# Pooled attention and a GELU feed-forward on one core: load shapes of v, order of the first batch's steps, order of the weight loads, and the last output tile in two parts

## The chip, the cores and the metric

The kernel runs on one core of a Trainium2 chip. The metric is the device time of one launch in microseconds. TensorE (PE in the profile) does the matmuls and the transposes, VectorE (DVE) and ScalarE (ACT) work on what it leaves in PSUM, and GpSimd (POOL) and SyncE (SP) mostly issue DMAs. ACT issues some DMAs as well.

## The reference

```python
# q, k, v: [8 batches, 8 heads, 576, 64] float32; w_in [512, 2048], w_out [2048, 512] float32
k_p = k.reshape(B, H, 72, 8, D).mean(axis=3)          # 8 neighbouring rows pooled
v_p = v.reshape(B, H, 72, 8, D).mean(axis=3)
scores = np.matmul(q, k_p.transpose(0, 1, 3, 2)) / np.sqrt(D)
attn = np.exp(scores - scores.max(-1)); attn /= attn.sum(-1)
x = np.matmul(attn, v_p).transpose(0, 2, 1, 3).reshape(4608, 512)
h = x @ w_in
g = 0.5 * h * (1 + np.tanh(c * (h + 0.044715 * h**3)))
out = g @ w_out                                        # [4608, 512] float32
```

## The kernel before

The 4608 rows of x are cut into nine groups of 512 (`GROUP`), and the attention of batch b + 1 is computed while group b goes through the feed-forward, so that x is always ready in SBUF, transposed, as `xT` (four blocks of 128 of its 512 features, `ko`, by 4608 rows). The schedule is written by hand: every engine works through its instructions in the order in which the program lists them.

**A group.** `p1_mm` (L336) computes h transposed, 16 blocks `fo` of 128 features with four matmuls of 512 columns each; `gelu` (L342, ACT) writes each block to `gT`. `p2_mm` (L345) multiplies four row tiles `r` of 128 rows by `w_out_b`, 16 matmuls of 512 columns each. `store` copies a row tile from its PSUM bank to SBUF on DVE (L350) and issues four output DMAs of 32 partitions by 2 KB (L356) on SP; for the very last row tile two of the four go out on ACT's queue. Between the `p2_mm` of a group stand the score matmuls (`qk`, L239), exponentials (`expo`, L247), value matmuls (`av`, L261) and divisions (`norm`, `mult`) of the next batch. In group 0 the first two row tiles use `w_out_b` a quarter at a time, eight matmuls for each quarter, because `w_out_b` is still arriving.

**The first batch** has no group to hide behind. Its steps stand ahead of group 0: pooling k (`k_steps`, L139), transposing k and q, the scores and exponentials of its eight half-batches, the pooling of v (`v_steps(0)`, L139, which adds the eight rows of each pool and writes `vz`), the denominators (`den0`, L289: matmuls with a block of ones), their reciprocals on ACT (`inverse0`, L294 and L296), the outputs (`av0`, L304, which reads `vz`) and the multiplication into `xT` on DVE (`mult0`, L308). `spin(n, bank)` (L362) puts n matmuls of zeros into a bank, whose only effect is on TensorE's time and clock. After the last `mult0` the matmuls of group 0 start.

**Loads.** `load_v(b, engs)` brings the first 64 of the 72 pools of each head to `vts`: 128 partitions, of which the lower 64 hold heads 0 to 3 and the upper 64 heads 4 to 7, with four slots of 512 values (8 rows of 64) in each. Before the change it is two DMAs of 64 partitions by four slots, the source being walked in the order pool, head, values. `load_k` brings k to `kts` and, with two small DMAs of 32 partitions (L76), the remaining eight pools of v, whose source is walked in the order pool (8), head (4), values. For batch 0, SP and ACT issue these loads. All other loads are issued by POOL, in this order: q of batch 0 in two halves, `w_in_b` in two halves (the DMA casts to bf16), k of batch 1 with its small parts (four DMAs), q of batch 1, v of batch 1 (two DMAs), the four quarters of `w_out_b`, then q of batch 2. Later batches are loaded by `load_next`, one per group.

Of the kernel before, what the change touches and what calls it, by code (L numbers as in the profile page):

```python
# [8 lines left out]
F32 = mybir.dt.float32  # L9
# [9 lines left out]
def kernel(  # L19
# [9 lines left out]
    nc = tc.nc  # L29
    B, H, S, D = q.shape  # L30
    Sp = S // 8
    N = B * S
    DM = H * D
    DF = moe_w_in.shape[1]
    KO = DM // 128
    FO = DF // 128
    T = S // 32
    TP = T // 2
    CH = S // 2
    GROUP = 512  # L40
    NG = N // GROUP
# [11 lines left out]
    opool = ctx.enter_context(tc.tile_pool(name="op", bufs=6))  # L53
# [4 lines left out]
    PS = psp.tile([128, 8, 512], F32, name="PS")  # L58
# [4 lines left out]
    vts = [consts.tile([128, 4, 512], F32, name=f"vt{i}") for i in range(2)]  # L63
# [12 lines left out]
            engs[-1].dma_start(out=kts[b % 2][32 * i:32 * i + 32, KR], in_=rows[64:, 4 * i:4 * i + 4])  # L76

    def load_v(b, engs):
        rows = v[b].rearrange("h (j l) d -> j h (l d)", l=8)
        for i in range(2):  # L80
            engs[i % len(engs)].dma_start(out=vts[b % 2][64 * i:64 * i + 64], in_=rows[0:64, 4 * i:4 * i + 4])  # L81

    def load_q(b, i0=0, i1=2):
        if b not in qs:
            qs[b] = qp.tile([128, 2, T * D], BF16, name="qb")
        nc.gpsimd.dma_start(  # L86
            out=qs[b][:, i0:i1],
            in_=q[b].rearrange("(i h) (p t) d -> (h p) i (t d)", i=2, t=T)[:, i0:i1])
# [3 lines left out]
    w_out_b = consts.tile([128, FO, DM], BF16, name="w_out_b")  # L92
# [15 lines left out]
    load_w_in(1)  # L108
    load_k(1, [nc.gpsimd])
    load_q(1)  # L110
    load_v(1, [nc.gpsimd])
    for i in range(4):
        nc.gpsimd.dma_start(out=w_out_b[:, 4 * i:4 * i + 4, :].rearrange("p j d -> p (j d)"), in_=w_out_v[:, i])  # L113
    gate = consts.tile([1, 2], BF16, name="gate")

# [81 lines left out]
    def trans_k(b, bank):  # L197
        trans_k_mm(b, bank)
        for e in range(2):
            trans_k_copy(b, e, bank)  # L200
# [31 lines left out]
    def pool_rows(pr):  # L232
        return Sp if pr < PR // 2 else 128
# [49 lines left out]
    def den0(c, pr, bank):  # L283
        for x in range(2):
            e = es[0, c, pr + x]
            n = pool_rows(pr)
            for y in range(2):
                one = ones[:n, pr // 2].rearrange("j a d -> j (a d)")[:, 64 - 64 * y:192 - 64 * y]
                nc.tensor.matmul(out=PS[:, bank + x, :CH], lhsT=one, rhs=e[:n, y, :],  # L289
                                 start=(y == 0), stop=(y == 1))  # L290

    def inverse0(c, pr, bank):
        ld = ep.tile([128, 2, CH], F32, name="ld0", bufs=1)
        nc.scalar.activation(out=ld, in_=PS[:, bank:bank + 2, :CH], func=ACT.Ln)  # L294
        rc = ep.tile([128, 2, CH], F32, name="rc0")
        nc.scalar.activation(out=rc, in_=ld, func=ACT.Exp, scale=-1.0)  # L296
        rcs[0, c, pr] = rc

    def av0(c, pr, bank):
        for x in range(2):  # L300
            e = es.pop((0, c, pr + x))
            n = pool_rows(pr)
            for y in range(2):
                nc.tensor.matmul(out=PS[:, bank + x, :CH], lhsT=window(vz[:n], 2 * (pr + x) + y),  # L304
                                 rhs=e[:n, y, :], start=(y == 0), stop=(y == 1))

    def mult0(c, pr, bank):
        nc.vector.tensor_tensor(out=xT[:, pr:pr + 2, c * CH:(c + 1) * CH], in0=PS[:, bank:bank + 2, :CH],  # L308
                                in1=rcs.pop((0, c, pr)), op=ALU.mult)
# [3 lines left out]
    def act_set(name):  # L313
        nc.scalar.preload_act_table_set(name)  # L314


    def x_bank(g):
        return g % 2
# [9 lines left out]
    def o_bank(g, r):  # L328
        return 1 - x_bank(g) if r % 2 == 0 else x_bank(g)

    gTs = {}
# [9 lines left out]
            gTs[g] = gpool.tile([128, FO, GROUP], BF16, name="gT")  # L341
        nc.scalar.activation(out=gTs[g][:, fo, :], in_=PS[:, h_bank(g, fo), :], func=ACT.Gelu_apprx_tanh)  # L342

    def p2_mm(g, r, fo):
        nc.tensor.matmul(out=PS[:, o_bank(g, r), :], lhsT=gTs[g][:, fo, r * 128:(r + 1) * 128], rhs=w_out_b[:, fo, :],  # L345
                         start=(fo == 0), stop=(fo == FO - 1))

    def store(g, r):
        osb = opool.tile([128, DM], F32, name="osb")
        nc.vector.tensor_copy(out=osb, in_=PS[:, o_bank(g, r), :])  # L350

        for n in range(4):
            b, c = divmod(g * GROUP + r * 128 + n * 32, S)
            rows = out[b * S:(b + 1) * S].rearrange("(p t e) d -> e t p d", t=TP, e=2)
            eng = nc.scalar if (g, r) == (NG - 1, 3) and n % 2 else nc.sync
            eng.dma_start(out=rows[c // CH, c % CH // 32], in_=osb[n * 32:(n + 1) * 32, :])  # L356


    def spin(n, bank):

        for _ in range(n):
            nc.tensor.matmul(out=PS[:, bank, :], lhsT=idle[:, 0:128], rhs=idle, start=True, stop=True)  # L362
# [24 lines left out]
    for h in range(H):  # L387
        i = h // 4
        nc.tensor.matmul(out=PS[64 - 64 * i:72 - 64 * i, 7, h * D:(h + 1) * D],
                         lhsT=identb[0:64, 32 * i + h % 4:32 * i + 32:4], rhs=kps[0][0:64, KR],  # L390
                         start=True, stop=True)
# [3 lines left out]
    for i in range(2):  # L395
        p = slice(64 - 64 * i, 72 - 64 * i)
        nc.vector.tensor_copy(out=vz[p, 4 * i:4 * i + 4, 0],
                              in_=PS[p, 7, 256 * i:256 * i + 256].rearrange("p (h d) -> p h d", d=D))
# [9 lines left out]
    for f in v_steps(0):  # L408
        f()
    inverse0(1, 0, 6)  # L410
    spin(4, 4)
    av0(0, 0, 4)
    mult0(0, 0, 4)
    den0(0, 2, 2)
    inverse0(0, 2, 2)
    av0(1, 0, 0)
    mult0(1, 0, 0)
    spin(3, 6)
    den0(1, 2, 6)
    inverse0(1, 2, 6)  # L420
    spin(3, 4)
    av0(0, 2, 4)
    mult0(0, 2, 4)
    spin(3, 0)
    av0(1, 2, 0)
    mult0(1, 2, 0)
    for t in kps:
# [12 lines left out]
    for g in range(NG):  # L440
        nb = g + 1 if g + 1 < B else None
        act_set(GELU_SET)

        def load_next():

            load_q(g + 2)
            trans_q_dma(g + 2)
            nc.gpsimd.tensor_copy(out=gate, in_=qTs[g + 2][0:1, 1, TP - 1, 0:2])  # L448
            load_k(g + 2, [nc.gpsimd])
            load_v(g + 2, [nc.gpsimd])  # L450

        if 0 < g and g + 2 < B:
            load_next()


        side = {fo: [] for fo in range(FO)}
        if nb is not None:
            kk = k_steps(nb)
            tk = [lambda: trans_k(nb, 4)]
            kk.append(lambda: v_moves(nb))  # L460
            vv = v_steps(nb)
            if g:
                plan = {2: kk[:1], 3: kk[1:], 7: vv[:1], 8: vv[1:], 9: tk}
            else:
                tq = [lambda a=a, i=i: trans_q(nb, *a, (5, 6, 7, 5)[i], nc.vector) for i, a in enumerate(QG)]
                plan = {0: kk, 12: tq[:1], 13: tq[1:2] + tk, 14: tq[2:3], 15: tq[3:] + vv}
            for fo, what in plan.items():
                side[fo] += what

        if g == 0:
            first = [(fo, ko) for ko in (2, 3) for fo in range(4)]
        else:
            late = 3
            rest = [fo for fo in range(4) if fo != late]
            first = [(fo, ko) for ko in range(3) for fo in rest]
            first += [(late, ko) for ko in range(3)]
            first += [(fo, 3) for fo in rest + [late]]
        for fo, ko in first:  # L480
            p1_mm(g, fo, ko)
        for fo in range(FO):
            if fo >= 4:
                for ko in range(KO):
                    p1_mm(g, fo, ko)
            gelu(g, fo)
            for s in side[fo]:
                s()

        if g == 0:  # L490
            load_next()


        todo = {}

        def at(m, f, *a):
            todo.setdefault(m, []).append((f, a))

        if nb is not None:
            act_set(EXP_SET)  # L500
            pos = (6, 14, 20, 27, 34, 41, 48, 55, 61)
            for i in range(len(ORDER) + 1):
                if i < len(ORDER):
                    at(pos[i], qk, nb, *ORDER[i], 2)
                if i:
                    a = (nb, *ORDER[i - 1], 4 + 2 * ((i - 1) % 2))
                    at(pos[i], av, *a)
                if i < len(ORDER):
                    at(pos[i], expo, nb, *ORDER[i], 2)
                if i:  # L510
                    at(pos[i], norm, *a)
                    at(min(pos[i] + 9, 62 if i < len(ORDER) else 65), mult, *a)
        seq = [(r, fo) for r in range(4) for fo in range(FO)]
        if g == 0:

            seq[:32] = [(r, 4 * f4 + f) for f4 in range(4) for r in range(2) for f in range(4)]
        for m, (r, fo) in enumerate(seq):
            for f, a in todo.pop(m, []):
                f(*a)
            p2_mm(g, r, fo)  # L520
            if fo == FO - 1:
                store(g, r)
        for m in sorted(todo):
            for f, a in todo[m]:
                f(*a)


# [28 lines left out]
```

The softmax here doesn't subtract the row's maximum and nothing guards it: scores larger than these inputs give would overflow.

## Time and profile before

| what | value |
|---|---|
| median of three runs | 308.79 us (308.76 to 308.96) |
| the profiled execution's own time | 308.29 us |
| its span, first to last instruction | 306.5 us |
| TensorE busy | 298.2 us (97%), 1518 matmuls |
| ACT, DVE, POOL busy | 219.0, 150.4, 36.3 us |
| DMA | 41.12 MB, mean 134 GB/s |
| first matmul of group 0 | 22.08 us |
| group 0, group 1, group 2, from first matmul to first matmul of the next | 33.70, 31.84, 31.84 us |

The profile is of one execution. Its own time is 1.79 us longer than its span, which is what lies before the first and after the last instruction, and it is 0.50 us below the median of the three runs. Times inside the profile are counted from the start of the span. A busy time of 97% on TensorE counts matmuls that overlap and the matmuls of zeros as well, so it is no measure of useful work; where the span can be shortened is read from what TensorE waits for and from the work that it does for no result.

### The profile page before, as it was taken

The page shows a single profiled execution, that of the slowest core. Times are in us where ns is not written, and L with a number is a line of the kernel's source. Part 1 is how long each engine was busy: PE and PEld are TensorE (multiplying, and loading weights), DVE is VectorE, ACT ScalarE, POOL GpSimd, SP SyncE. Part 2 cuts the span into 40 slices and gives each one's busy share as a digit, 9 for nine tenths or more (in the row PEclk, how much of TensorE's full clock was granted, in tenths as well). Part 3 has the DMA queues.
Part 4 walks back from the last instruction along what each step waited for, and adds up shares of the span by engine and source line. Part 5 has one row for each costly group of instructions (what it writes and reads, how often), then busy time and mean ns, then how long its engine had stood idle before and what let it go on. Part 6 is the DMA issues. An engine that isn't in the chain of part 4 may idle for free.

```text
span 306.5 us, 4325 instructions
## 1 busy us (share of the span) xinstructions
PE 298.2 (97%) x1518; PEld 157.4 (51%) x1548; DVE 150.4 (49%) x334; ACT 219.0 (71%) x402; POOL 36.3 (12%) x69
## 2 busy tenths in 40 slices
PE   8999999999999999999999999999999999999994
PEld 3555555555555555555555555555555555445441
DVE  5868557573677057806681559245933630110021
ACT  1686679868987798779977998789868987206400
POOL 7103002305004000220014000400000000000000
PEclk9999999999999999999999999999999999999999
DMA  7999996987957952596159725662101210121022
GB/s 225 266 257 253 214 186 137 299 176 177 269 146 167 247 122 51 114 282 156 34 112 266 168 56 106 200 151 71 35 1 36 63 41 2 34 70 34 2 70 68
DMA packets 30359, 41.12 MB, mean 134 GB/s; under 512 B 18113, under 2 KB 18113, under 8 KB 29441
## 3 DMA queue, kind: packets, MB, share of 16 engines
q0 software_dynamic: 7856, 25.43, 34.9%
q1 hardware_dynamic: 21888, 14.09, 19.2%
q10 hardware_dynamic: 592, 1.31, 1.2%
q8 instruction: 12, 0.20, 0.3%
q14 instruction: 11, 0.08, 0.1%
HBM read 36.70 MB, written 9.44 MB: 151 GB/s over the span
## 4 chain that ended last, share of the span: by engine, by line
PE 83%; DMA 12%; POOL 1%; issue 1%; ACT 0%; DVE 0%; POOLq 0%
PE PS L345 38%; PE PS L336 36%; DMA kt<-in_k_dram 7%; DMA w_out_b<-in_moe_w_out_dram 5%; PE PS L239 4%; PE PS L261 4%; PE PS L174 1%; POOL w_in_b L105 0%; POOL qb L86 0%; POOL w_out_b L113 0%; DVE osb L350 0%; ACT e L247 0%; ACT ld L269 0%; ACT ld L268 0%; POOL identb masks.py:199 0%
## 5 line engine op out<-in xcount | busy, mean ns | idle before, releaser
L345 PE MATMUL PS<-w_out_b,gT 128*128 128x512 bf16 x560 | 134.2, 379 | 0.9
L336 PE MATMUL PS<-xT,w_in_b 128*128 128x512 bf16 x563 | 126.2, 379 | 0.6
L342 ACT ACTIVATE gT<-PS 128x512 bf16<-128x512 f32 x144 | 81.1, 604 | 47.5 <-PE PS L336 47.4
L336 PEld LDWEIGHTS <-w_in_b 128*128 128x128 bf16 x576 | 64.7, 113 | 57.2
L345 PEld LDWEIGHTS <-gT 128*128 128x128 bf16 x576 | 56.1, 97 | 56.7 <-issue 1.1
L350 DVE COPY osb<-PS 128x512 f32<-128x512 f32 x36 | 24.9, 691 | 98.3 <-PE PS L345 95.3
L279 DVE TENSOR_TENSOR xT<-PS,rc 64x288 bf16<-64x288 f32 x112 | 51.0, 455 | 31.6 <-ACT rc L271 29.3
L247 ACT ACTIVATE e<-PS 72x576 bf16<-72x576 f32 (+1 forms) x64 | 41.0, 646 | 9.1 <-PE PS L239 8.2
L239 PE MATMUL PS<-qT,kT 128*72 128x288 bf16 (+1 forms) x128 | 25.9, 286 | 0.9 <-ACT qT L214 0.6
L271 ACT ACTIVATE rc<-ld 128x288 f32<-128x288 f32 x56 | 24.8, 443 | 1.8
L314 ACT ACT_TABLE_LOAD x17 | 21.8, 1283 | 4.3 <-issue 4.1
L268 ACT ACTIVATE ld<-PS 64x288 f32<-64x288 f32 x56 | 22.8, 407 | 1.3
L269 ACT ACTIVATE ld<-PS 64x288 f32<-64x288 f32 x56 | 22.5, 402 | 1.3
L261 PE MATMUL PS<-e,vp 72*128 72x288 bf16 (+1 forms) x112 | 23.1, 286 | 0.0
L139 DVE TENSOR_TENSOR kt<-kt 128x1280 f32<-128x1280 f32 (+5 forms) x18 | 18.8, 1044 | 5.5 <-DMA kt<-in_v_dram 2.6
L239 PEld LDWEIGHTS <-kT 128*72 128x72 bf16 (+1 forms) x128 | 13.2, 105 | 15.2 <-DVE qT L216 1.2
L448 POOL COPY gate<-qT 1x2 bf16<-1x2 bf16 x6 | 1.0, 174 | 140.0 <-DMA qT<-qb 140.0
L139 DVE TENSOR_TENSOR vt<-vt 128x1024 f32<-128x1024 f32 (+1 forms) x16 | 15.3, 956 | 1.8 <-DMA vt<-in_v_dram 1.5
L184 DVE COPY kT<-PS 64x288 bf16<-64x288 bf16 (+2 forms) x48 | 13.0, 319 | 6.2 <-PE PS L174 6.1
L362 PE MATMUL PS<-idle 128*128 128x512 bf16 x39 | 11.9, 447 | 1.2 <-DVE idle L127 1.2
L261 PEld LDWEIGHTS <-vp 72*128 72x128 bf16 (+1 forms) x112 | 11.0, 98 | 3.8
L81 POOL DMA_DIRECT2D vt<-in_v_dram x14 | 9.0, 655 | 7.5 <-DMA w_in_b<-in_moe_w_in_dram 5.5
(47 smaller groups left out, 90.0 us busy)
## 6 DMA issues: line engine op xcount, KB each, us to landing
out_dram<-osb SPq DMA_DIRECT2D x142, 64.0 KB
kt<-in_k_dram POOLq DMA_DIRECT2D x7, 1024.0 KB, 6.2
vt<-in_v_dram POOLq DMA_DIRECT2D x14, 512.0 KB, 8.6
qb<-in_q_dram POOLq DMA_DIRECT2D x7, 576.0 KB, 11.6
w_in_b<-in_moe_w_in_dram POOLq DMA_DIRECT2D x2, 1024.0 KB, 16.7
w_out_b<-in_moe_w_out_dram POOLq DMA_DIRECT2D x4, 512.0 KB, 13.9
kt<-in_k_dram POOLq DMA_DIRECT2D x7, 128.0 KB, 5.9
kt<-in_v_dram POOLq DMA_DIRECT2D x14, 64.0 KB, 5.7
```

Of the source, the lines that this page charges most:

```text
L139: nc.vector.tensor_tensor(out=o, in0=a, in1=b, op=ALU.add)
L239: nc.tensor.matmul(out=PS[:n, bank + e, :CH].rearrange("j (t p) -> j t p", p=32), lhsT=kTs[b % 2][c][:, h, :n], rhs=qTs[b][:, h // 4, :, h ...
L247: nc.scalar.activation(out=e[:n], in_=PS[:n, bank:bank + 2, :CH], func=ACT.Exp, scale=1.0 / 64.0)
L261: nc.tensor.matmul(out=PS[:, bank + x, :CH], lhsT=window(vps[b % 2][:n], 2 * pr + x), rhs=e[:n, x, :], start=True, stop=True)
L268: nc.scalar.activation(out=ld[0:64], in_=PS[64:128, bank, :CH], func=ACT.Ln)
L269: nc.scalar.activation(out=ld[64:128], in_=PS[0:64, bank + 1, :CH], func=ACT.Ln)
L271: nc.scalar.activation(out=rc, in_=ld, func=ACT.Exp, scale=-1.0)
L279: nc.vector.tensor_tensor(out=xT[rows, pr, col:col + CH], in0=PS[rows, bank + x, :CH], in1=rc[rows], op=ALU.mult)
L336: nc.tensor.matmul(out=PS[:, h_bank(g, fo), c0:c1], lhsT=w_in_b[fo // 8][:, ko, q * 512 + j:(q + 1) * 512:4], rhs=xT[:, ko, r0 + c0:r0 + c ...
L342: nc.scalar.activation(out=gTs[g][:, fo, :], in_=PS[:, h_bank(g, fo), :], func=ACT.Gelu_apprx_tanh)
L345: nc.tensor.matmul(out=PS[:, o_bank(g, r), :], lhsT=gTs[g][:, fo, r * 128:(r + 1) * 128], rhs=w_out_b[:, fo, :], start=(fo == 0), stop=(fo ...
L350: nc.vector.tensor_copy(out=osb, in_=PS[:, o_bank(g, r), :])
```

## The change

Four places are edited.

1. `load_v` becomes four DMAs, one for each slot of `vts`. Each has 128 partitions by 2 KB as its destination, and its source is walked in the order half (heads h and h + 4), pool (64), values. For batch 0 SP issues slots 0 and 2 and ACT slots 1 and 3. For the other batches POOL issues all four.
2. POOL issues the first quarter of `w_out_b` ahead of v of batch 1, not after it.
3. In the steps of the first batch, `den0` and `inverse0` of the half-batches (0, 2) and (1, 2) move ahead of `av0(0, 0)` and `av0(1, 0)`. The spins between them go from 4, 3, 3 and 3 matmuls to 2, 2 and 2.
4. The last row tile of the last group is computed as two accumulations, columns 0 to 383 in its bank and columns 384 to 511 in bank 4, each followed by its own copy and four output DMAs. Those of the first part all go out on SP; of the second part two on SP and two on ACT.

```diff
     def load_v(b, engs):
-        rows = v[b].rearrange("h (j l) d -> j h (l d)", l=8)
-        for i in range(2):
-            engs[i % len(engs)].dma_start(out=vts[b % 2][64 * i:64 * i + 64], in_=rows[0:64, 4 * i:4 * i + 4])
+        rows = v[b].rearrange("(i h) (j l) d -> h i j (l d)", i=2, l=8)
+        for h in range(4):
+            engs[h % len(engs)].dma_start(out=vts[b % 2][:, h], in_=rows[h, :, 0:64])
...
     load_q(1)
-    load_v(1, [nc.gpsimd])
     for i in range(4):
+        if i == 1:
+            load_v(1, [nc.gpsimd])
         nc.gpsimd.dma_start(out=w_out_b[:, 4 * i:4 * i + 4, :].rearrange("p j d -> p (j d)"), in_=w_out_v[:, i])
...
-    def p2_mm(g, r, fo):
+    def p2_mm(g, r, fo, bank, c0=0, c1=DM):
...
-    def store(g, r):
-        osb = opool.tile([128, DM], F32, name="osb")
-        nc.vector.tensor_copy(out=osb, in_=PS[:, o_bank(g, r), :])
+    def store(g, r, bank, c0=0, c1=DM):
+        if (g, r) not in osbs:
+            osbs[g, r] = opool.tile([128, DM], F32, name="osb")
+        osb = osbs[g, r]
+        nc.vector.tensor_copy(out=osb[:, c0:c1], in_=PS[:, bank, c0:c1])
...
-            eng = nc.scalar if (g, r) == (NG - 1, 3) and n % 2 else nc.sync
-            eng.dma_start(out=rows[c // CH, c % CH // 32], in_=osb[n * 32:(n + 1) * 32, :])
+            eng = nc.scalar if c1 == DM and c0 and n % 2 else nc.sync
+            eng.dma_start(out=rows[col // CH, col % CH // 32, :, c0:c1], in_=osb[n * 32:(n + 1) * 32, c0:c1])
...
     inverse0(1, 0, 6)
-    spin(4, 4)
+    spin(2, 4)
+    den0(0, 2, 2)
+    inverse0(0, 2, 2)
+    spin(2, 4)
     av0(0, 0, 4)
     mult0(0, 0, 4)
-    den0(0, 2, 2)
-    inverse0(0, 2, 2)
+    den0(1, 2, 6)
+    inverse0(1, 2, 6)
     av0(1, 0, 0)
     mult0(1, 0, 0)
-    spin(3, 6)
-    den0(1, 2, 6)
-    inverse0(1, 2, 6)
-    spin(3, 4)
     av0(0, 2, 4)
     mult0(0, 2, 4)
-    spin(3, 0)
+    spin(2, 0)
     av0(1, 2, 0)
     mult0(1, 2, 0)
...
-        seq = [(r, fo) for r in range(4) for fo in range(FO)]
+        seq = [(r, fo) for r in range(4 if g + 1 < NG else 3) for fo in range(FO)]
...
+    for c0, c1, bank in ((0, 384, o_bank(g, 3)), (384, DM, 4)):
+        for fo in range(FO):
+            p2_mm(g, 3, fo, bank, c0, c1)
+        store(g, 3, bank, c0, c1)
```

More of the change, by code (lines that the diff above doesn't have):

```diff
@@ L342, in gelu @@
         nc.scalar.activation(out=gTs[g][:, fo, :], in_=PS[:, h_bank(g, fo), :], func=ACT.Gelu_apprx_tanh)
-    def p2_mm(g, r, fo):
-        nc.tensor.matmul(out=PS[:, o_bank(g, r), :], lhsT=gTs[g][:, fo, r * 128:(r + 1) * 128], rhs=w_out_b[:, fo, :],
-                         start=(fo == 0), stop=(fo == FO - 1))
-    def store(g, r):
-        osb = opool.tile([128, DM], F32, name="osb")
-        nc.vector.tensor_copy(out=osb, in_=PS[:, o_bank(g, r), :])
+    def p2_mm(g, r, fo, bank, c0=0, c1=DM):
+        nc.tensor.matmul(out=PS[:, bank, c0:c1], lhsT=gTs[g][:, fo, r * 128:(r + 1) * 128],
+                         rhs=w_out_b[:, fo, c0:c1], start=(fo == 0), stop=(fo == FO - 1))
+    osbs = {}
+    def store(g, r, bank, c0=0, c1=DM):
[3 more added lines that the diff above has]
+        nc.vector.tensor_copy(out=osb[:, c0:c1], in_=PS[:, bank, c0:c1])
         for n in range(4):
-            b, c = divmod(g * GROUP + r * 128 + n * 32, S)
+            b, col = divmod(g * GROUP + r * 128 + n * 32, S)
             rows = out[b * S:(b + 1) * S].rearrange("(p t e) d -> e t p d", t=TP, e=2)
-            eng = nc.scalar if (g, r) == (NG - 1, 3) and n % 2 else nc.sync
-            eng.dma_start(out=rows[c // CH, c % CH // 32], in_=osb[n * 32:(n + 1) * 32, :])
+            eng = nc.scalar if c1 == DM and c0 and n % 2 else nc.sync
+            eng.dma_start(out=rows[col // CH, col % CH // 32, :, c0:c1], in_=osb[n * 32:(n + 1) * 32, c0:c1])
     def spin(n, bank):
@@ L519 @@
                 f(*a)
-            p2_mm(g, r, fo)
+            p2_mm(g, r, fo, o_bank(g, r))
             if fo == FO - 1:
-                store(g, r)
+                store(g, r, o_bank(g, r))
         for m in sorted(todo):
```

## The prediction

> **What bounds the kernel now.** I read the page first: TensorE is busy for 97% of the span, and the chain of waits that ended last runs 83% on it. Only two DMAs stand in that chain, both before 44.03 us:
>
> ```profile
> 4.55 21.57 DMA kt<-in_k_dram
> ...
> 27.46 16.53 DMA w_out_b<-in_moe_w_out_dram
> 43.99 0.04 issue
> 44.03 0.81 PE PS L345 x3
> ```
>
> The loads of POOL's queue land one after another, and the last quarter of w_out lands just when TensorE needs it. From group 1 on nothing but TensorE decides. So an edit pays only before 55.78 us (the start of group 1) or after the last matmul. The timeline of TensorE shows the first batch's end:
>
> ```profile
> 15.98 1.03 PE L362 MATMUL PS<-idle 128*128 128x512 bf16 x4
> 17.18 0.66 PE L304 MATMUL PS<-e,vz 72*128 72x288 bf16 x4 [0.17 <-DVE vz L139]
> ```
>
> Here `av0` waits for v: DVE starts the pooling of v at 14.72 and TensorE follows 2.46 us later. Group 0 starts at 22.08. Thus v of batch 0 had landed by 14.72; how much later the new loads land is the question that decides. The queues, in 0 to 15 us and then in two windows of 2 us (6 to 8, 9 to 11; columns: packets, MB, share of 16 engines):
>
> ```profile
> q1 hardware_dynamic: 496, 1.18, 24.1%
> q10 hardware_dynamic: 496, 1.18, 21.1%
> ...
> q10 hardware_dynamic: 51, 0.09, 12.2%
> ...
> q0 software_dynamic: 103, 0.19, 50.4%
> q1 hardware_dynamic: 102, 0.21, 30.3%
> q10 hardware_dynamic: 102, 0.21, 26.5%
> ```
>
> q1 is SP, q10 ACT, q0 POOL. Each of q1 and q10 moved 128 packets of 4 KB (k), 64 of 2 KB (the small parts) and 256 of 2 KB (v), together 448; 48 more are the completion packets. SP issued three DMAs, so 16 each. ACT issued four: k and v take 32, and 16 remain for the two small ones, eight each. These two (L76) have 32 partitions as destination but pool (8) outermost in the source. In 6 to 8 us, when they run, q10 moves 51 packets, half of the 102 that it moves later: eight engines, the same for both.
>
> **What the Trainium skill says.** "DMA: Bandwidth & Descriptors", section "Why a DMA increments its semaphore by 16 and not by 1": a DMA runs on the largest number of engines up to 16 that divides the slowest dimension of both its source and its destination; from SP and ACT it takes the lowest-numbered ones, and only these post a completion. The eights above agree. The same page, "Queues, rings and completion order": an engine serves its queues in turn, packet by packet; 103, 102 and 102 packets agree. "TensorE: Matmul & The Clock Gate", Part 1: after an idle window of about 3.4 us the array's clock is halved for about as long. The granted clock column shows 1.00 throughout, but the first 22 spins took 7.13 us where 22 at 0.216 take 4.75, so 2.38 us were lost: it agrees in effect.
>
> **The change part by part.**
>
> 1. *v by four DMAs.* The new destination has 128 partitions, but the source counts half (2) first. Two is the largest number that divides both, so by the rule each runs on two engines, and the four of batch 0 on the same two. These get 512 packets / 2 = 256 of v, 128 from each of SP and ACT, where they had 16 from each. SP has 4 more ahead (the rest of k), ACT 8 (the small parts): take 132 turns of all three queues. In 9 to 11 us a turn took 2 us x 16 / 102 = 0.314 us; 132 turns take 41.4. In that time POOL's queue goes through 132 packets as well, of which some 16 (k of batch 1, the first quarter of w_out) take about 0.31 in place of 0.16 us: +2.4. Start at 5.8 us, when k was in (DVE's first L139), about 1.4 for the last landing and its semaphore: **v is there at 51 us**, not before 14.72. From below: were SP and ACT served first, 264 turns at 0.095 and 0.083 (share x 32 us / packets) take 23.5, so 30 us. From above: with no overlap of packets, and POOL's all at their own lengths (0.19 q, 0.17 w_in, 0.31 k, 0.32 w_out), 57.
>
>  From there to group 0: DVE's pooling 2.46; then av0, den0(1, 2), av0, av0, two spins and av0, five times 0.49 and 0.43, 2.89 us; TensorE has idled over 30 us, so the cold clock costs 2.38. 51 + 7.73 = 58.7 against 22.08: **+36.7 us**. Behind `av0` in TensorE's order stands everything, so nothing covers this. ACT's and DVE's own work of the first batch needs some 11 us and waits at no cost; if ACT is held up while issuing its two DMAs (the small ones took 0.68 and 1.38 us to issue, the others 0.43 and 0.70), that too is hidden.
> 2. *Later denominators ahead, fewer spins.* The part after `av0(0, 0)` shrinks from 4.90 us (17.18 to 22.08) to 2.89, which the sum above holds already. If v came in time, it would give 1.41: two spins, den0(0, 2) and two spins end at 17.33, 0.15 late, and the last spins wait for `mult0(1, 0)` to free bank 0, 0.45.
> 3. *w_out's first quarter ahead of v of batch 1.* POOL has eight DMAs outstanding: its ninth waits for the first, and so on (vt for the second half of q, w_out for w_in and k). Two more issues (0.64 us each) shift the sequence: the last quarter waits for q of batch 1, the next q for w_out's first quarter. None of these comes late, as the weights are needed 37 us later. Group 0 takes 33.70 us, group 1 31.84; 18 more transposes at 0.056 explain 1.0, and the 0.86 left is the wait for w_out, which disappears: **-0.9**.
>
>  Later batches: POOL's v DMAs on two engines each, 64 packets at 0.157 us, take some 10 us. Batch 3's are issued at 98.25 and read at 124.5: hidden. Batch 2's were read as they landed (DVE waited 1.5 us); their q now lands earlier relative to TensorE. I take 0, bounds 0 and +3.
> 4. *Last row tile in parts.* TensorE: 16 matmuls of 384 and 16 of 128 columns stream 16 x 512 in all; nine transposes of 128 columns with their weight loads come at 0.056 us each, so 0. The tail:
>
> ```profile
> 302.11 0.69 DVE L350 COPY osb<-PS 128x512 f32<-128x512 f32 x1 [2.76 <-PE PS L345]
> 302.84 0.85 ACTq L356 DMA_DIRECT2D out_dram<-osb  x2
> ...
> 292.47 11.14 SPq L356 DMA_DIRECT2D out_dram<-osb  x14
> ```
>
> The last copy shrinks to about 0.25 (estimate from its width), -0.45. But SP now issues six DMAs at 0.42: four from 301.85 on (the first part ends 16 x 0.056 = 0.9 earlier, its copy takes 0.53), so it is free at 303.55 and done with the last two at 304.4; before, at 303.6. The last issue ends 0.8 later, and the data is a quarter: **+0.6**, bounds -0.5 and +0.9.
>
> Sum: 308.29 (the profiled execution: span 306.5 and 1.79 around it) + 36.7 - 0.9 + 0.6 = 344.7. The median is 0.50 above that execution: **345 us**.
>
> **Rivals.**
>
> *A, spread as meant (faster).* The four DMAs run on all 16 engines, because what the instruction carries isn't the source as written. For: 64-partition loads of v cost POOL's queue more than their bytes (last w_out 44.0, first w_out 36.6, so 2.47 us a quarter; from q of batch 1 at 30.3 to 44.0 are 13.7, of which 9.9 are w_out and 3.8 v, against about 2.5 for as many bytes of w_out's source), so up to 1.3 us to win. Against: the eights. Group 0 starts 1.41 earlier, and the last w_out must come earlier by as much to keep it; it decides from 1.3 us on. 308.8 - 1.4 + 0.6 = 308.0 if v still lands by 14.7; 306.5 if also the tail improves; 309.4 if w_out comes no earlier and the tail loses.
>
> *B, two engines for each DMA, but different ones.* Each pair then has 64 packets of v: 64 turns of two queues at 0.25 = 16, from 7 us on, v at 24 or 25. Group 0 at about 32.5, +10.4: 319 us. Against: the two small DMAs shared one set of eight.
>
> *C, SP and ACT served ahead of POOL.* v at 30 us, +15.6: 324 us. Against: the equal counts in 9 to 11 us.
>
> **How the numbers follow.** A change of 0.2% (0.6 us) is about what a measurement of this kernel can tell from none. My forecast has 0.73, B 0.08, C 0.07, A 0.12. Of A 0.08 is faster, 0.02 the same, 0.02 slower. So faster 0.08, same 0.02, slower 0.90. The range takes in B and C from below; above, v at 57 us (+6), 3 for batch 2 and up to 5 for a longer cold clock and POOL's longer packets: 318 to 359.
>
> **What would show it.** In the profile after: 80 - 16 + 2 x 2 = 68 completion packets and not 96 on q10 over the whole span if two engines serve each (before: 592 - 512 = 80; the two DMAs of v replace one); DMA share falling once 14 engines are done while q1 and q10 still move packets at 40 us; `vz` or the first L139 on vt waiting some 35 us for in_v; the first L336 near 59 us; no wait for w_out in group 0; SP's last issue ending after ACT's. It is wrong if v is there at 15 us, and the sum is wrong if group 0 starts in time but another group is long.

## The result and the profile after

The changed kernel takes 347.26 us (median of four runs, 346.25 to 347.50) against 308.77 before: ratio 1.1243, 95% interval 1.1217 to 1.1269. The forecast was 345. The profiled execution has a span of 345.7 us and a time of 347.47.

The chain that ended last, in order of time (start, duration, what), now has one piece that was not there:

```profile
5.93 46.67 DMA vt<-in_v_dram
...
52.63 1.24 DVE vt L141
...
54.62 0.43 DVE vz L141
...
55.09 1.14 PE PS L306 x4
```

v of batch 0 is there at 52.63 us; before, DVE started on it at 14.72 without a wait:

```profile
14.72 1.95 DVE L139 TENSOR_TENSOR vt<-vt 128x1024 f32<-128x1024 f32 x2
```

TensorE and ACT stand behind it. The page's 40 slices show the hole and the lower clock in it, first before (slices of 7.7 us, TensorE and its clock), then after (8.6 us):

```profile
PE   8999999999999999999999999999999999999994
...
PEclk9999999999999999999999999999999999999999
...
PE   8910006999999999999999999999999999999994
...
PEclk9975555999999999999999999999999999999999
DMA  7993693039859825964793498278320121022022
```

ACT's queue over the whole span, and then all three queues between 9 and 11 us and between 31 and 33 us (packets, MB, share of 16 engines):

```profile
q10 hardware_dynamic: 580, 1.21, 0.9%
...
q0 software_dynamic: 195, 0.40, 104.8%
q1 hardware_dynamic: 14, 0.03, 4.1%
q10 hardware_dynamic: 13, 0.02, 2.9%
...
q0 software_dynamic: 11, 0.07, 8.3%
q1 hardware_dynamic: 10, 0.02, 2.7%
q10 hardware_dynamic: 10, 0.02, 2.6%
```

ACT's queue carries 512 packets of data as before, so 68 completion packets: 16 for k, 8 and 8 for the small parts, 32 for the last stores, and 2 and 2 for v. Between 9 and 11 us SP and ACT move 14 and 13 packets where they moved 102 each; POOL's queue takes over all that is free. One completion for each engine serving a DMA is what the count shows. That the same two engines served all four is read from 31 to 33 us, when POOL has little else to move: the three queues move 11, 10 and 10 packets, and all of these together take 13.6% of the time of 16 engines, which is 2.2 engines (at full load the shares add up to somewhat over 100%, as between 9 and 11 us). Two pairs would have been busy at twice that share. A turn, one packet from each queue, then takes 2 x 2 / 10 = 0.40 us on two engines, and the mean packets of the three queues are 0.24, 0.09 and 0.08 us long, 0.41 together.

Where the 39.2 us of span went, from first to last:

| stretch | before | after | difference |
|---|---|---|---|
| to DVE's start on v | 14.72 | 52.63 | +37.91 |
| from there to `av0` | 2.46 | 2.46 | 0 |
| `av0` to the start of group 0 | 4.90 | 5.74 | +0.84 |
| group 0 | 33.54 | 33.55 | +0.01 |
| start of group 1 to the last copy of a row tile | 246.49 | 246.54 | +0.05 |
| from there to the end | 4.39 | 4.78 | +0.39 |

Group 0 is counted here to the first matmul of group 1, at 55.62 us before and 94.38 after. The 33.70 us in the table ahead of the prediction end at 55.78, where the last matmul of group 0 ends (54.97 + 0.81); the matmuls overlap, as the lines of before show:

```profile
54.97 0.81 PE L345 MATMUL PS<-w_out_b,gT 128*128 128x512 bf16 x3
55.62 4.70 PE L336 MATMUL PS<-xT,w_in_b 128*128 128x512 bf16 x20
```

### The profile page after: what moved, and what is told of

Read it like the earlier page. It is cut to its first block, busy times and chain, and to the rows that moved or that the text cites. A ratio compares the mean times of both kernels' runs of the same rounds, so it can differ in the third digit from the quotient of the medians.

```text
span 345.7 us, 4373 instructions
## 1 busy us (share of the span) xinstructions
PE 300.4 (87%) x1528; PEld 159.0 (46%) x1557; DVE 150.5 (44%) x335; ACT 218.9 (63%) x402; POOL 50.3 (15%) x83
## 3 DMA queue, kind: packets, MB, share of 16 engines
q0 software_dynamic: 20624, 25.53, 33.6%
## 4 chain that ended last, share of the span: by engine, by line
PE 82%; DMA 15%; DVE 1%; issue 1%; ACT 0%
PE PS L338 36%; PE PS L347 35%; DMA vt<-in_v_dram 14%; PE PS L241 4%; PE PS L263 4%; DMA kt<-in_k_dram 1%; PE PS L306 1%; PE PS L176 1%; DVE vt L141 1%; PE PS L206 0%; PE PS L368 0%; PE PS L291 0%; ACT e L249 0%; DVE vz L141 0%; ACT ld L271 0%
## 5 line engine op out<-in xcount | busy, mean ns | idle before, releaser
L347 PE MATMUL PS<-w_out_b,gT 128*128 128x512 bf16 (+2 forms) x577 | 133.9, 373 | 0.7
L347 PEld LDWEIGHTS <-gT 128*128 128x128 bf16 x592 | 57.1, 98 | 55.6 <-issue 0.4
L356 DVE COPY osb<-PS 128x512 f32<-128x512 f32 (+2 forms) x37 | 25.1, 677 | 100.5 <-PE PS L347 80.9
L306 PE MATMUL PS<-e,vz 72*128 72x288 bf16 (+1 forms) x16 | 4.4, 445 | 36.9 <-DVE vz L141 36.9
L298 ACT ACTIVATE rc<-ld 128x576 f32<-128x576 f32 x4 | 2.7, 682 | 38.3 <-DVE xT L310 38.3
L82 POOL DMA_DIRECT2D vt<-in_v_dram x28 | 22.5, 827 | 22.9 <-DMA w_in_b<-in_moe_w_in_dram 19.7
L306 PEld LDWEIGHTS <-vz 72*128 72x128 bf16 (+1 forms) x16 | 2.2, 145 | 39.0 <-DVE vz L141 37.4
## 6 DMA issues: line engine op xcount, KB each, us to landing
qb<-in_q_dram POOLq DMA_DIRECT2D x7, 576.0 KB, 12.8
```

The costliest lines, as they stand in the source:

```text
L82: engs[h % len(engs)].dma_start(out=vts[b % 2][:, h], in_=rows[h, :, 0:64])
L347: nc.tensor.matmul(out=PS[:, bank, c0:c1], lhsT=gTs[g][:, fo, r * 128:(r + 1) * 128], rhs=w_out_b[:, fo, c0:c1], start=(fo == 0), stop=(fo ...
L356: nc.vector.tensor_copy(out=osb[:, c0:c1], in_=PS[:, bank, c0:c1])
```

## The experiments

**The loads of v alone decide.** First the changed kernel with only `load_v` put back, run as v_old_rest_new:

```diff
-        rows = v[b].rearrange("(i h) (j l) d -> h i j (l d)", i=2, l=8)
-        for h in range(4):
-            engs[h % len(engs)].dma_start(out=vts[b % 2][:, h], in_=rows[h, :, 0:64])
+        rows = v[b].rearrange("h (j l) d -> j h (l d)", l=8)
+        for i in range(2):
+            engs[i % len(engs)].dma_start(out=vts[b % 2][64 * i:64 * i + 64], in_=rows[0:64, 4 * i:4 * i + 4])
```

> The changed kernel with the loads of v as before (two DMAs of 64 partitions, pool outermost in the source); everything else of the change stays. Theory (two engines serve each of the new loads of v): all 16 engines serve v again, it is there by 14.7 us, group 0 starts near 20.7 us; the last quarter of w_out still lands near 44 us, so what the earlier start wins is waited for there, and the tail costs 0.4: 309.2 us. Rival 1 (the order of the steps or of the weight loads makes the loss): it stays near 347. Rival 2 (the earlier start is kept): 307.8.

Measured: 308.81 us, ratio to the kernel before 0.9991 (0.9975 to 1.0008). Then v_new_only, the kernel before with only the same edit the other way round:

> The kernel before with the new loads of v and nothing else. Theory: v of batch 0 is there near 52.6 us as in the changed kernel, group 0 starts 2.46 + 4.90 us later plus 2 to 3.4 for the cold clock, near 63; no wait for w_out in group 0; 348 to 350 us. Rival (it takes the moved weight load or the new order as well): well below 347.

Measured: 345.78 us, in one run. The loss is in `load_v`, with the other three edits or without. The size expected was 2 to 4 us too high. v was there at 50.66 us and not near 52.6, and group 0 started at 60.09. In the changed kernel the first quarter of w_out stands in POOL's queue ahead of v of batch 1, and its eight packets per engine of 0.32 us each, 2.6 us, could make the 2 us. That is not shown: in v_new_only too POOL issued all four quarters, from 37.01 to 44.42 us, before v of batch 0 was there. The 2 us, between one profile of each kernel, stay open.

**It is the count outermost in the source.** Batch 0's v by four DMAs of 128 partitions with 4 heads outermost (v_four_engines) or 8 (v_eight_engines), everything else as before:

```diff
+        if b == 0:   # v_four_engines
+            rows = v[b].rearrange("(i h) (j l) d -> h i j (l d)", i=4, l=8)
+            for n in range(4):
+                engs[n % 2].dma_start(out=vts[0][:, n], in_=rows[n % 2, :, n // 2 * 32:n // 2 * 32 + 32])
...
+        if b == 0:   # v_eight_engines
+            rows = v[b].rearrange("h (j l) d -> h j (l d)", l=8)
+            for n in range(4):
+                engs[n % 2].dma_start(out=vts[0][:, n], in_=rows[:, 16 * n:16 * n + 16])
```

> The kernel before, but batch 0's v comes by four DMAs of 128 partitions whose source counts 4 heads outermost, then 32 pools; the same bytes in packets of 2 KB, but they land in other places, so x of batch 0 is another than the reference's. Theory: four engines serve each, 128 packets of v per engine, 64 from SP and 64 from ACT; 68 to 72 turns of 0.314 us from 5.8 us on and 1.4 for the landing: v at 29 us, group 0 near 39 to 40, 325 to 327 us; 48 - 16 + 8 = 40 completion packets of q10 ahead of the stores. Rival 1 (partitions or the number of DMAs matter, not the count outermost): v at 52 us, 348. Rival 2 (the engines aren't the same for the four DMAs): v at 15 to 18 us, 309 to 312.

> As before, with 8 heads outermost in the source of batch 0's v, then 16 pools; again the bytes land in other places and x of batch 0 is another than the reference's. Theory: eight engines, 64 packets of v per engine, 36 to 40 turns of 0.314 us: v at 19 to 20 us, group 0 near 27 to 28, 313 to 315 us; 48 completion packets of q10. Rival 1: 348. Rival 2: 309.

Measured: 328.08 and 315.42 us, one run each. DVE's start on v, with the wait before it in brackets, first with four, then with eight:

```profile
32.37 1.95 DVE L144 TENSOR_TENSOR vt<-vt 128x1024 f32<-128x1024 f32 x2 [17.32 <-DMA vt<-in_v_dram]
...
19.77 1.95 DVE L144 TENSOR_TENSOR vt<-vt 128x1024 f32<-128x1024 f32 x2 [4.39 <-DMA vt<-in_v_dram]
```

ACT's queue over the whole span, in the same order:

```profile
q10 hardware_dynamic: 584, 1.31, 1.3%
...
q10 hardware_dynamic: 592, 1.31, 1.2%
```

Taking away 512 packets of data, and 16 + 8 + 8 + 32 completions for k, the small parts and the stores, leaves 8 and 16 for ACT's two DMAs of v: four and eight engines each. The destinations have 128 partitions in all of these, the number of DMAs is four, the bytes and the packets are the same. The nearest run with a count of 2 is v_new_only: like these two it is the kernel before with other loads of v, though in all batches. So v is there at 50.66, 32.37 and 19.77 us for 2, 4 and 8. With 5.8 us for the start and 1.4 for the landing as in the prediction, that is 0.329, 0.360 and 0.331 us for each of 132, 70 and 38 turns. All are longer than the 0.314 expected, and with four engines v came 3.4 us later than expected; why the turns were longest there, these runs don't show.

**The same four slots on all engines.** v_eight_halves is the changed kernel with each of the four DMAs cut into two of 64 partitions, so that the source counts 64 pools outermost:

```diff
-            engs[h % len(engs)].dma_start(out=vts[b % 2][:, h], in_=rows[h, :, 0:64])
+            for i in range(2):
+                engs[h % len(engs)].dma_start(out=vts[b % 2][64 * i:64 * i + 64, h], in_=rows[h, i, 0:64])
```

> The changed kernel with each of the four DMAs of v cut into its two halves: eight DMAs of 64 partitions by 2 KB, the pool (64) outermost in the source. Same bytes, same slots, same packets of 2 KB, more issues. Theory: 64 divides by 16, so 16 engines serve each and 48 more completion packets appear per four of them; v is there near 15 to 16 us, 309 to 310 us. Rival (one slot for each DMA, or many DMAs, is what is slow): near 347 or above.

Measured: 310.89 us, ratio 1.0069 (1.0045 to 1.0093). ACT's queue has 640 packets, that is four times 16 for its share of v, and v's wait is gone: all of q1's and q10's packets of the loads, 544 each, moved before 15 us. The 36 us are recovered. What is left over the expectation comes with another wait, which ACT's timeline shows (the profiled execution took 312.41 us; the runs lie between 308.46 and 312.58):

```profile
3.32 6.98 ACTq L82 DMA_DIRECT2D vt<-in_v_dram  x4
```

ACT is held for 7 us over its four issues, where its one DMA of v took 0.70 before; its first copy of q starts at 11.63 us in place of 9.10. TensorE waits 3.07 us for it, its granted clock is 0.50 from 11 to 21 us where it stood at 1.00 before, group 0 starts at 26.51, and group 1 at 59.61 in place of 55.62. The runs bear it out: ten of the eleven have a mean clock of 0.984 to 0.993 and take 310.08 us or more; the one with 1.000 takes 308.46. So the longer hold on ACT costs time where the clock falls with it.

**POOL's later loads of v.** v_old_batch0 is the changed kernel with only batch 0's v loaded as before:

```diff
+        if b == 0:
+            rows = v[b].rearrange("h (j l) d -> j h (l d)", l=8)
+            for i in range(2):
+                engs[i].dma_start(out=vts[0][64 * i:64 * i + 64], in_=rows[0:64, 4 * i:4 * i + 4])
+            return
```

> The changed kernel with batch 0's v loaded as before (two DMAs of 64 partitions); all other batches keep the four DMAs, issued by POOL. Theory: the 38 us come from batch 0 alone. What is left: v of batch 1 puts 64 packets of 2 KB, some 5.5 to 10 us, on eight of the engines ahead of the last three quarters of w_out, in place of 3.8 on all, so the last quarter lands 2 to 6 us later than 44 us and group 0 waits for it; later batches are hidden: 311 to 315 us. Rival (POOL's two-engine loads are hidden everywhere): 309.2.

Measured: 314.45 us, ratio 1.0176 (1.0149 to 1.0203). TensorE's waits (total, times, longest) name the place:

```profile
PE PS L352 <- DMA w_out_b<-in_moe_w_out_dram: 5.2, 1, 5.2
```

v_old_rest_new differs from it in the later loads of v alone and takes 308.81 us. So the two-engine loads cost a second time, 5.6 us in batch 1, where they stand ahead of three quarters of w_out. In the changed kernel this cost is hidden behind the larger wait. DVE also waits 4.79 us for v of batch 2, and no wait of TensorE follows from it.

**The other edits by themselves.** order_only is the kernel before with the third edit, tail_parts_only with the fourth; their edits are those parts of the change's diff.

> The kernel before with the new order of denominators and outputs and with the fewer spins, and nothing else. Theory: group 0 starts 1.4 us earlier, near 20.7, but the last quarter of w_out lands at 44.0 as before and takes the gain: 308.6 to 308.9. Rival (TensorE alone decides): 307.4.

> The kernel before with the last row tile in two parts and nothing else. Theory: SP's six issues end after ACT's two, and the last data leaves later: +0.4 us as in the changed kernel's tail, 309.2. Rival (the smaller last copy decides): -0.4, 308.4.

Measured: 308.65 us, ratio 0.9987 (0.9972 to 1.0002), and 308.69, ratio 0.9998 (0.9984 to 1.0012). The order does what it says, group 0 starts at 20.74 us and not at 22.08, and gives it back (group 1 starts at 55.89 and not at 55.62), as TensorE's waits show in order_only:

```profile
PE PS L345 <- DMA w_out_b<-in_moe_w_out_dram: 1.2, 2, 0.9
```

These two waits are for earlier quarters of w_out. The last quarter decides: it lands at 44.26 us in order_only, at 43.99 before and at 43.54 in v_old_rest_new, and group 1 starts 11.6 us after it in all three (55.89, 55.62 and 55.16). The tail in parts moves the time by less than these runs resolve: from the last copy to the end its profile has 4.4 us, against 4.39 before and 4.78 in the changed kernel.

**A version that beats both.** If the queue ahead of w_out holds the gain of the order back, taking v of batch 1 out of that queue should release it. order_v1_on_sp is order_only with one line changed; order_v1_k1_on_sp moves k of batch 1 as well; order_v1_on_sp_tail adds the two-part tail to the first, with the stores of both parts spread over SP and ACT.

```diff
-    load_k(1, [nc.gpsimd])
+    load_k(1, [nc.sync])      # order_v1_k1_on_sp only
...
-    load_v(1, [nc.gpsimd])
+    load_v(1, [nc.sync])      # all three
...
+            eng = nc.scalar if (g, r) == (NG - 1, 3) and n % 2 else nc.sync      # order_v1_on_sp_tail, both parts
```

> The kernel before with the new order of denominators and outputs, and v of batch 1 (two DMAs of 64 partitions, as before) issued by SP behind batch 0's v. Theory: with v on all engines what holds the gain of the order back is the queue of loads ahead of the last quarter of w_out. v of batch 1 takes POOL's queue 3.8 us there; from SP its 2 KB packets take 0.095 us each, 32 per engine, 3.0 us, between 12 and 20 us, where w_in has some 4 us of slack. The last quarter of w_out lands about 1 us sooner, near 43, and the new order keeps about 1 us: 307.5 to 308.2. Rival (w_in's first half comes too late beside it): group 0 starts later than 20.8 us, no gain.

> As order_v1_on_sp, with k of batch 1 on SP as well. Theory: k's packets are long on either queue, so the total stays, but 2.5 to 3 us more run ahead of w_in; its first half then lands near 23 us, after group 0 could start at 20.7: no gain over the kernel before, or a loss of up to 2 us: 308 to 311. Rival (w_in's slack is enough): 307.5.

> As order_v1_on_sp, with the last row tile in two parts, and the stores of both parts spread over SP and ACT, two and two. Theory: SP's last issue then ends 0.4 us after the last copy in place of 2.0, so the tail is 0.3 to 0.5 us shorter than with one part: 307.1 to 307.8. Rival (the tail is set by the last data's way out and not by the issues): equal to order_v1_on_sp.

Measured: 307.17 us, ratio 0.9947 (0.9935 to 0.9959); 308.75, ratio 0.9996 (0.9985 to 1.0008); and 306.84, ratio 0.9935 (0.9917 to 0.9953). The first and the last are each a little below what was expected. In order_v1_on_sp the last quarter of w_out lands 12.8 us after its issue at 29.32, at 42.1 us, TensorE has no wait for w_out left, and group 1 starts at 54.15 in place of 55.62. With k moved too, group 0 starts at 23.19 in place of 21.05. The expected wait for w_in is there, in TensorE's first matmuls of group 0, but only 0.48 us long:

```profile
23.19 11.41 PE L336 MATMUL PS<-xT,w_in_b 128*128 128x512 bf16 x51 [0.48 <-DMA w_in_b<-in_moe_w_in_dram]
...
16.60 1.95 DVE L139 TENSOR_TENSOR vt<-vt 128x1024 f32<-128x1024 f32 x2 [1.44 <-DMA vt<-in_v_dram]
```

More of it comes from v of batch 0, which the expectation had not counted: DVE waits 1.44 us for it, and the first `av0` starts at 19.06 in place of 17.58.

The tail with its stores spread takes 3.9 us from the last copy's start to the end where order_v1_on_sp takes 4.3, but the intervals of the two overlap: that the tail gains is not settled.

## Why the prediction was right

Point by point, by its own steps.

1. *v by four DMAs.* Right in mechanism. The 68 completion packets on q10 came out exactly; the runs with 4 and 8 confirm that the count outermost sets the engines. The term was 51 us against 52.63 measured: a turn of the three queues took 0.344 us on average and not 0.314. I had added 2.4 us in all for POOL's longer packets; the turns measured 4 us more than 132 x 0.314, so that allowance came out short. It counted k of batch 1 and one quarter of w_out. POOL issued the other three quarters at 37.57 to 44.86 us, before v was there, and between 42 and 46 us SP and ACT moved 18 packets each: 2 x 4 / 18 = 0.44 us a turn. The lower bound (SP and ACT first) is excluded by the 14 and 13 packets between 9 and 11 us, where it asks for 22 of each, and the rival of different engines by these and by the shares between 31 and 33 us.
2. *From v to group 0.* DVE's 2.46 us came out as written. The rest was put at 5.27 (2.89 and 2.38 for the cold clock) and took 5.74, and the clock was still half for about 0.9 us of group 0:

```profile
55.00:56.00 1.00, 0.91 (x4) 0.50 0.12 11
...
60.00:61.00 1.00, 1.00 (x6) 0.50 0.12 25
61.00:62.00 1.00, 1.00 (x5) 0.63 0.14 29
62.00:63.00 1.00, 0.95 (x5) 1.00 0.12 25
```

   (Columns of this table by stage: us, TensorE busy and its matmuls, granted clock, DMA share, GB/s.) The clock was down for some 6.7 us after the restart (55.09 to 61.74, from the 0.63) and not 4.8 (twice the 2.38 lost) as at the kernel's start, nor the 3.4 that the prediction quotes. At half the clock 6.65 us lose 3.3, of which 0.45 fall into group 0. In v_new_only it was back some 4.3 us after the restart at 53.12. The length of the cold stretch differs between two kernels with the same hole; what sets it, these runs don't show.
3. *The wait for w_out disappears, -0.9.* The wait went, but group 0 took 33.55 us after 33.54. Up to its first matmul with w_out it took 15.55 us and not 15.10, 0.45 more for the half clock; from there to group 1 it took 18.00 and not 18.44. So the wait was worth 0.44 us and not 0.86, and the cold clock, which the prediction had ending before group 0, took that back. The five kernels v_new_only, v_four_engines, v_eight_engines, v_eight_halves and order_v1_on_sp, without a wait for w_out and at full clock, confirm the size: their group 0 takes 33.10 us. The prediction had put to the wait all that the 18 transposes did not explain. Of its 0.86 us, 0.16 come from reading 55.78 as the start of group 1, and 0.26 stay with group 0 without any wait (33.10 - 31.84 - 1.0); what they are, these runs don't show.
4. *The tail, +0.6.* The signs were right: the last copy takes 0.29 us (0.25 estimated), and SP, with six issues, ends after ACT. In the changed kernel's timelines of DVE, ACT and SP:

```profile
340.92 0.29 DVE L356 COPY osb<-PS 128x128 f32<-128x128 f32 x1 [0.34 <-PE PS L347]
341.24 0.84 ACTq L362 DMA_DIRECT2D out_dram<-osb  x2
...
338.14 5.10 SPq L362 DMA_DIRECT2D out_dram<-osb  x10
```

   SP's last issue ends at 343.24, 1.2 us after ACT's last. The end moved by 0.39 us in this profile, and tail_parts_only shows no change that its interval (0.5 us less to 0.4 us more) can resolve. The term was too large.
5. *Batch 2's v, 0 with bounds 0 and +3.* Zero: groups 1 to 8 took 0.05 us more.

The sum was 36.7 - 0.9 + 0.6 = 36.4 us; measured were 39.2 of span. Four terms missed by 1.6 (v), 0.5 (the restart), 0.9 (group 0) and -0.2 (the tail), 2.8 in all. The misses were small beside the one term that decides, and they did not cancel.

Of rival A one part is now known by v_old_rest_new and order_only: even with v in time, the order and the moved quarter of w_out win nothing that the runs can tell. In order_only the last quarter of w_out came 0.27 us later than before. In v_old_rest_new it came 0.45 us sooner, and group 1 started 0.46 sooner; one profile can't say whether moving the first quarter did that. Its condition, that the last quarter lands 1.3 us sooner, was met by order_v1_on_sp (42.1 against 43.99), and there the gain came.

## What to carry to other kernels

A DMA's spread over the engines follows from the counts outermost in both of its patterns: 128 partitions on one side help nothing when the other side starts with a count of 2, and the completion packets of SP's and ACT's queues tell how many engines serve each DMA. Read the counts before a load is reshaped, and prefer DMAs whose outermost counts are multiples of 16 to one that only looks wider. When work is moved earlier and the time stays, look for the next transfer that lands just in time, and shorten the queue in front of it.

## What the runs showed that I had not expected

- A two-engine DMA issued by POOL adds small packets. POOL's queue moved 20,624 packets in all against 7,856 before, with almost the same bytes (25.53 and 25.43 MB). Without the 14 old loads of v (128 + 16 packets each) 5,840 remain; the 28 new ones then have 528 each: 64 of 4 KB, 16 completions and 448, which is 32 for each of the other 14 engines. The count fits, and the pages show that they are small: packets under 512 B went from 18,113 to 30,920. The 64 packets of v are of 4 KB; the prediction and the expectation of v_old_batch0 had counted twice as many of 2 KB. Which engines the packets ran on is not in the profile.
- In these traces ACT's queue takes four DMAs and holds its fifth until the first has landed. The changed kernel's second DMA of v on ACT is its fifth: the two issues take 3.13 us, and the load of the activation table behind them, released by k's landing, starts at 6.50 us in place of 4.06. What sets the limit of four is not in the profile. It cost nothing here; with the eight halves, seven DMAs on ACT, the hold was 6.98 us.
